# Four of the eight w2_out operand pairs are converted between the attention stages, and output stores are issued two steps later

## The chip, the cores and the metric

The kernel runs on one core of a Trainium2 chip. The metric is the time of one execution on the device in microseconds (us). Five engines matter here: TensorE (PE, with its weight loads shown apart as PEld), VectorE (DVE), ScalarE (ACT), the queue that issues most transfers (SP), and the 16 DMA engines that carry them. Each engine takes its instructions in the order in which they stand in its own queue, and waits for others by semaphores.

## The reference, cut to what matters

```python
# attention through 32 memory slots (4 batches, 8 heads, 576 positions, 64 wide)
a = exp(phi - max(phi, axis=2)); a = a / (sum(a, axis=2) + 1e-9)
k_m = einsum('bhsm,bhsd->bhmd', a, k); v_m = einsum('bhsm,bhsd->bhmd', a, v)
attn = softmax(q @ k_m.T / 8)            # over the 32 slots
x = (attn @ v_m) laid out as 2304 x 512
# gated layer: 512 -> 1536 -> 512
x = ((x @ w_a) * (x @ w_b)) @ w_out
# leaky layer: 512 -> 2048 -> 512
h = x @ w2_in
return maximum(0.01 * h, h) @ w2_out     # 2304 x 512, fp32
```

## The kernel before, in words

All products run as fp32r passes on TensorE: each operand is split into a high and a low part, and three of the four products of parts are summed. A weight tile of 128 rows is loaded into one of five staging tiles (`stage0` to `stage4`, `NS = 5`), two ACT instructions (lines 263 and 267) and one DVE instruction (line 275) bring it into fp32, and ACT and DVE then make the high and the low part.

**First phase, planned.** Its steps are collected in a `Plan` (line 41): each has an engine, a cost in us, what it must follow, and perhaps a staging tile or a PSUM bank that it takes and gives back. `order` (line 79) simulates the engines and puts the steps into one order by due time; `early` makes a step due earlier. The order fixes every engine's queue, SP's included. The phase has eight units: the four batches with the first six column blocks of the gated layer, then the four with the other six. A unit is 144 matmuls `ab` (line 793), a few `wp` (line 742), and 144 matmuls `x1p` (line 850). The attention of batch b+1 (ten small matmul groups with DVE and ACT work between them) lies inside the `x1p` of unit b, so units 0 to 2 hold the attention stages of batches 1 to 3. Units 4 to 7 also hold conversions of the second layer's weights.

**Second phase, in program order and then scheduled.** Both products of the leaky layer are made by a 7-product scheme on 2x2 blocks. Its operands (sums and differences of blocks, with high and low part) are made by `plan_pair` (line 930): "in" pairs from `w2_in`, "out" pairs from `w2_out`, eight of each. A pair loads two weight tiles, converts them, forms four sums, splits seven operands, and stores them in four parts to a scratch area in DRAM (line 1014). The second phase reads them back: `h` matmuls (line 1241, six per step) take `ring` tiles (line 1048), `o` matmuls (line 1330, nine per step) take `w2o` tiles (line 1303) through staging tiles, two halves in each, up to six steps ahead.

The 2304 rows and 16 blocks give 24 quads of `h` products, in six chunks of 28 steps. Chunk 0 has `h` alone; in chunks 1 to 5 a step is six `h` matmuls of the chunk and nine `o` matmuls of the chunk before; a last chunk has `o` alone. Its final product, 36 matmuls, stands on line 1311. ACT and DVE take each `h` result out of PSUM (lines 1258 to 1272), form the sums `g` (line 1284) and split them into `S` (lines 1293 and 1294).

In the kernel before, the eight "in" pairs and the first four "out" pairs are in the plan (units 4 to 7); the last four "out" pairs (`LATE = 4`) are not. A second small plan, `late_plan` (line 1372), orders their steps, and the loop over the second phase emits them step by step beside chunks 0 and 1:

```python
tempo += 0.9
while late and late[0].start < tempo:
    late.popleft().emit()
```

They use staging tiles for the loads and the tiles `R0`, `R1`, `B4` and `G5` for the results. Until they are done, `w2o` has two of its four staging tiles, `S` four of its seven places. An output block is stored (line 1364) as soon as its sum stands; each store is six transfers on SP.

Of the kernel before, what the change touches and what calls it, by code (L numbers as in the profile page):

```python
# [176 lines left out]
def kernel(  # L177
# [39 lines left out]
    NP = NM // 2  # L217
# [6 lines left out]
    LATE = 4  # L224
# [69 lines left out]
    def plan_conv(c, before, users, due=1e9):  # L294

        h = Hold("stage", 1)
        load = plan.add(DMA, 1.46, lambda: c.load(f"stage{h.place}"), take=h)
# [14 lines left out]
    def plan_wab(f):  # L312

        pair = f // 2
        if f % 2 == 0:
            wab_slot[pair] = plan.slot(f"A{pair % NA}")
        for n, src in enumerate((w_a, w_b)):

            def make(n=n):
                if pair not in wab_t:  # L320
                    wab_t[pair] = keep.tile([128, KD, 2, 2, 128], F32, tag=f"A{pair % NA}", name="wab")
                return wab_t[pair][:, :, f % 2, n, :]

            view = src[:, f * 128:(f + 1) * 128].rearrange("(t p) c -> p t c", p=128)
            plan_conv(Conv(("wab", f, n), view, make, 1), *wab_slot[pair])

    def plan_wo(f):
# [6 lines left out]
        plan_conv(Conv(("wo", f), w_out[f * 128:(f + 1) * 128, :], make, 2), before, users)  # L334
# [10 lines left out]
    def plan_att(b):  # L345
# [155 lines left out]
        for g in range(NG):  # L501
# [22 lines left out]
            for n in range(2):  # L524
# [30 lines left out]
                else:  # L555
# [6 lines left out]
                    vb_end[b, g] = add(DVE, t_dve(128), values, [s_kvt], give=[hold_t], early=5.0 if b else 0.0)  # L562
# [123 lines left out]
        for i in range(3):  # L686
# [24 lines left out]
            ends += [s_hi, add(DVE, t_dve(384), low, [s_hi], give=[hold], early=5.0)]  # L711
# [165 lines left out]

    units = [(b, range(f, f + FH)) for f in (0, FH) for b in range(B)]
    n_first = B

# [6 lines left out]
    for u, (b, fs) in enumerate(units):  # L887
# [29 lines left out]
    OPS = (("A11", "B11"), ("S2", "T2"), ("A12", "B21"), ("S3", "T3"), ("S1", "T1"), ("A22", "T4"), ("S4", "B22"))  # L917
    PARTS = (("A11", "S2"), ("A12", "S3"), ("S1", "A22"), ("S4",))
    scr = ctx.enter_context(tc.tile_pool(name="scratch", bufs=1, space=bass.MemoryType.DRAM))
    a_scr, o_scr, a_kept = {}, {}, {}  # L920

    O_OPS = (("A11", "B11", "y"), ("S3", "T3", "z"), ("S2", "T2", "y"), ("A22", "T4", "z"), ("S1", "T1", "y"),
             ("A12", "B21", "x"), ("S4", "B22", "z"))
    O_PARTS = (("B11", "T3"), ("T2", "T4"), ("T1", "B21"), ("B22",))
    IN_SUMS = ((("S1", (1, 0), (1, 1), ALU.add), ("S2", "S1", (0, 0), ALU.subtract)),
               (("S3", (0, 0), (1, 0), ALU.subtract), ("S4", (0, 1), "S2", ALU.subtract)))
    OUT_SUMS = ((("T1", (0, 1), (0, 0), ALU.subtract), ("T2", (1, 1), "T1", ALU.subtract)),
                (("T3", (1, 1), (0, 1), ALU.subtract), ("T4", (1, 0), "T2", ALU.subtract)))

    def plan_pair(plan, kind, mp, due, places=("R0", "R1")):  # L930

        c, js = {}, []
        inner = kind == "in"
        sums, parts, letter = (IN_SUMS, PARTS, "A") if inner else (OUT_SUMS, O_PARTS, "B")
        names = [x for ops in sums for op in ops for x in op[1:3] if not isinstance(x, str)]
        names += [(int(x[1]) - 1, int(x[2]) - 1) for part in parts for x in part if x[0] == letter]
        holds = [Hold("stage", sum(x[0] == i for x in names)) for i in range(2)]
        convs = []
        for i in range(2):
            m = 2 * mp + i  # L940
            if inner:
                view = w2_in[:, m * 128:(m + 1) * 128].rearrange("(t p) c -> p t c", p=128)
            else:
                view = w2_out[m * 128:(m + 1) * 128, :]
            conv = Conv(("w2" + kind, m), view, None, 2)
            convs.append(conv)
            load = plan.add(
                DMA, 1.46, lambda conv=conv, h=holds[i]: conv.load(f"stage{h.place}"), [s_p2], take=holds[i], due=due
            )
            v = plan.add(ACT, t_act(512), conv.high_word, [load])  # L950
            z = plan.add(ACT, t_act(512), conv.low_word, [load])
            js.append(plan.add(DVE, t_dve(512), conv.join, [v, z]))

        def a(i, k):
            w = convs[i].hw.bitcast(F32)
            if inner:
                return w.rearrange("p (a k c) -> p a k c", a=2, k=2)[:, :, k]
            return w[:, 256 * k:256 * k + 256].rearrange("p (a c) -> p a c", a=2)

        def src(op):  # L960
            if op in c:
                return c[op]
            return a(int(op[1]) - 1, int(op[2]) - 1)

        made = {}
        for n, ops in enumerate(sums):
            before, users = plan.slot(f"ob{n}")
            for i, (name, x, y, op) in enumerate(ops):

                def add(name=name, x=x, y=y, op=op, n=n, i=i):  # L970
                    if i == 0:
                        c["t", n] = keep.tile([128, 2, 2, 128], F32, tag=f"ob{n}", name="S")
                    x, y = (c[z] if isinstance(z, str) else a(*z) for z in (x, y))
                    c[name] = c["t", n][:, i]
                    dve.tensor_tensor(out=c[name], in0=x, in1=y, op=op)

                need = [made[z] for z in (x, y) if isinstance(z, str)]
                give = [holds[z[0]] for z in (x, y) if not isinstance(z, str)]
                uses = [users] + [made[z].users for z in (x, y) if isinstance(z, str) and made[z].users is not users]
                made[name] = plan.add(DVE, t_dve(256), add, js + before + need, give=give, uses=uses)  # L980
                made[name].users = users
        for i, part in enumerate(parts):
            tag = f"X{i}" if inner else places[i % len(places)]
            before, users = plan.slot(tag)
            lows = []
            for o, name in enumerate(part):

                def parted(o, x, i=i):
                    t = c["out", i][:, o]
                    return t[:, :, x] if inner else t[:, x].rearrange("p (a c) -> p a c", a=2)  # L990

                def high(i=i, o=o, name=name, tag=tag, part=part, parted=parted):
                    if o == 0:
                        shape = [128, len(part), 2, 2, 128] if inner else [128, len(part), 2, 256]
                        pool = p2[0] if tag[0] in "XR" else keep
                        c["out", i] = pool.tile(shape, F32R, tag=tag, name="a_out" if inner else "w2o")
                    act.activation(out=parted(o, 0), in_=src(name), func=ACTF.Copy)

                def low(o=o, name=name, parted=parted):
                    dve.tensor_tensor(out=parted(o, 1), in0=src(name), in1=parted(o, 0).bitcast(F32), op=ALU.subtract)  # L1000

                direct = name[0] == letter
                need = js if direct else [made[name]]
                uses = [users] if direct else [users, made[name].users]
                hi = plan.add(ACT, t_act(256), high, need + before + lows, uses=uses)
                lows.append(plan.add(
                    DVE, t_dve(256), low, [hi], uses=uses, give=[holds[int(name[1]) - 1]] if direct else ()
                ))

            def store(i=i, part=part):  # L1010
                shape = [128, len(part), 2, 2, 128] if inner else [128, len(part), 2, 256]
                t = scr.tile(shape, F32, tag=f"{kind}{mp}_{i}", name="a_scr")
                (a_scr if inner else o_scr)[mp, i] = t
                dma.dma_start(out=t, in_=c["out", i].bitcast(F32))

            kept = plan.add(DMA, 0.73 * len(part), store, lows, uses=[users], due=due)
            if inner:
                a_kept[mp, i] = kept
        return holds

    for mp in range(NP):
        due = clock[0] - 20.0 + 2.0 * mp
        plan_pair(plan, "in", mp, due)
        if mp < NP - LATE:
            plan_pair(plan, "out", mp, due + 6.0)
# [473 lines left out]
```

## Time and profile before

| what | value |
|---|---|
| time, median of 3 executions | 771.82 us (771.09 to 773.05) |
| profiled execution, its own time | 773.19 us |
| its span, first to last instruction | 771.4 us |
| granted TensorE clock, mean | 0.997 |
| PE busy | 753.5 us (98%) |
| PEld busy | 709.5 us (92%) |
| DVE busy | 549.4 us (71%) |
| ACT busy | 424.0 us (55%) |
| DMA, mean | 227 GB/s |

The profiled execution took 1.37 us more than the median; 1.8 us of its time lie outside the span. The first `h` matmul starts at 397.16 us, the second phase takes the rest. Busy shares are means over stages with different limits, so the stages have to be read apart.

### The profile page before, as it was taken

What the parts mean: (1) busy time and instruction counts of PE and PEld (TensorE: products, weight loads), DVE (VectorE), ACT (ScalarE), POOL (GpSimd) and SP (SyncE); (2) the same over time, 40 slices, a digit from 0 to 9 for tenths busy, and PEclk for the clock granted to TensorE, in tenths of its full rate; (3) what the DMA queues carried; (4) which work ended last, traced back from release to release, by engine and by line L of the source; (5) the groups of instructions that cost most, each with busy time, mean ns of one, the idle gap of its engine ahead of it and who ended that gap; (6) DMA issues with size and microseconds to landing.
All of it is one profiled execution on the core that took longest, in us unless ns stands there. A gap on an engine that the chain in (4) does not pass through costs nothing.

```text
span 771.4 us, 16541 instructions
## 1 busy us (share of the span) xinstructions
PE 753.5 (98%) x6462; PEld 709.5 (92%) x6462; DVE 549.4 (71%) x1082; ACT 424.0 (55%) x894; POOL 1.2 (0%) x9
## 2 busy tenths in 40 slices
PE   8999999999999999999999999999999999999996
PEld 5599899898998989898998899999999999999995
DVE  5794764646828988997987767976755966756683
ACT  4897444544948676666665455633444733444440
POOL 0000000000000000000000000000000000000000
PEclk9999999999999999999999999999999999999998
DMA  9986305102705877679759999987897777886375
GB/s 305 350 289 230 102 2 187 31 2 82 237 13 164 285 275 278 215 250 342 266 202 308 285 361 331 332 268 234 277 311 251 254 249 241 266 318 211 124 235 133
DMA packets 86925, 175.41 MB, mean 227 GB/s; under 512 B 8000, under 2 KB 35136, under 8 KB 86848
## 3 DMA queue, kind: packets, MB, share of 16 engines
q1 hardware_dynamic: 86608, 174.16, 66.9%
q8 instruction: 51, 0.84, 0.4%
q10 hardware_dynamic: 240, 0.20, 0.1%
q14 instruction: 26, 0.21, 0.1%
HBM read 140.25 MB, written 34.08 MB: 226 GB/s over the span
## 4 chain that ended last, share of the span: by engine, by line
PE 88%; DMA 6%; ACT 2%; DVE 2%; SPq 1%; issue 1%; ACTq 0%; DVEq 0%
PE o L1330 22%; PE ab L793 20%; PE h L1241 19%; PE x1p L850 18%; PE wp L742 3%; DMA stage<-in_moe_w_out_dram 2%; DMA w2o<-a_scr 2%; DMA stage<-in_moe_w_a_dram 1%; PE sc L625 1%; PE km L481 1%; DMA a_scr<-w2o 1%; PE qT L597 1%; PE warm L1179 1%; PE o L1311 1%; SPq L1364 1%
## 5 line engine op out<-in xcount | busy, mean ns | idle before, releaser
L1330 PE MATMUL o<-w2o,S 128*128 128x256 f32 x1476 | 196.8, 282 | 1.7 <-DMA w2o<-a_scr 1.7
L1330 PEld LDWEIGHTS o<-w2o,S 128*128 128x128 f32 x1476 | 191.7, 190 | 2.3 <-DMA w2o<-a_scr 2.3
L793 PEld LDWEIGHTS ab<-AT,W 128*128 128x128 f32 x1152 | 153.9, 188 | 14.4 <-issue 5.9
L850 PE MATMUL x1p<-G,wo 128*128 128x288 f32 x1152 | 164.3, 298 | 0.0
L850 PEld LDWEIGHTS x1p<-G,wo 128*128 128x128 f32 x1152 | 154.7, 188 | 6.7 <-issue 3.0
L793 PE MATMUL ab<-AT,W 128*128 128x288 f32 x1152 | 159.2, 297 | 1.0 <-DVE W L761 0.7
L1241 PE MATMUL h<-T,ring 128*128 128x384 f32 x720 | 144.3, 337 | 2.8 <-ACT g L1251 1.6
L1294 DVE TENSOR_TENSOR S<-g,S 128x384 fp32r<-128x384 f32 x168 | 92.6, 556 | 73.5 <-ACT S L1293 73.1
L1293 ACT ACTIVATE S<-g 128x384 fp32r<-128x384 f32 x168 | 87.2, 521 | 102.1 <-PE o L1330 99.6
L1241 PEld LDWEIGHTS h<-T,ring 128*128 128x128 f32 x720 | 121.5, 189 | 5.0 <-ACT g L1251 2.5
L1241 PE MATMUL h<-B,ring 128*128 128x384 f32 x288 | 58.7, 338 | 1.7 <-ACT sums L1258 1.6
L815 DVE TENSOR_TENSOR g<-a_sb,ab 128x288 f32<-128x288 f32 x96 | 42.9, 452 | 20.7 <-PE ab L793 15.8
L1284 DVE TENSOR_TENSOR g<-g 128x384 f32<-128x384 f32 x96 | 52.4, 554 | 3.4 <-ACT g L1251 2.4
L263 ACT ACTIVATE stage<-stage 128x512 f32<-128x512 f32 x68 | 46.4, 683 | 13.6 <-DMA stage<-in_moe_w_out_dram 8.3
L1241 PEld LDWEIGHTS h<-B,ring 128*128 128x128 f32 x288 | 48.3, 188 | 3.0 <-ACT sums L1258 2.3
L810 ACT COPY a_sb<-ab 128x288 f32<-128x288 f32 x96 | 38.0, 396 | 15.1 <-PE ab L793 14.3
L267 ACT ACTIVATE stage<-stage 128x512 int32<-128x512 uint32 x68 | 46.1, 678 | 0.0
L761 DVE TENSOR_TENSOR W<-wp,W 128x512 fp32r<-128x512 f32 x48 | 32.4, 687 | 18.7 <-ACT W L755 17.9
L829 ACT ACTIVATE G<-g 128x576 fp32r<-128x576 f32 x48 | 32.9, 686 | 18.3 <-DVE g L815 18.3
L833 DVE TENSOR_TENSOR G<-g,G 128x576 fp32r<-128x576 f32 x48 | 36.2, 755 | 7.8 <-ACT G L829 7.3
L755 ACT ACTIVATE W<-wp 128x512 fp32r<-128x512 f32 x48 | 27.8, 597 | 24.3 <-PE wp L742 14.8
L1351 DVE TENSOR_TENSOR C<-C,o 128x768 f32<-128x768 f32 x32 | 30.2, 953 | 12.6 <-PE o L1330 11.7
(108 smaller groups left out, 658.6 us busy)
## 6 DMA issues: line engine op xcount, KB each, us to landing
w2o<-a_scr SPq DMA_DIRECT2D x168, 256.0 KB, 4.0
ring<-a_scr SPq DMA_DIRECT2D x72, 512.0 KB, 5.1
stage<-in_moe_w_out_dram SPq DMA_DIRECT2D x28, 512.0 KB, 5.7
a_scr<-a_out SPq DMA_DIRECT2D x24, 512.0 KB, 5.5
a_scr<-w2o SPq DMA_DIRECT2D x24, 512.0 KB, 5.3
stage<-in_moe_w_in_dram SPq DMA_DIRECT2D x16, 512.0 KB, 4.9
stage<-in_moe_w_a_dram SPq DMA_DIRECT2D x12, 512.0 KB, 5.6
stage<-in_moe_w_b_dram SPq DMA_DIRECT2D x12, 512.0 KB, 5.7
```

The source lines that it names most:

```text
L263: act.activation(out=x, in_=x, func=ACTF.Prelu, scale=2.0 ** -112, alpha=2.0 ** 32)
L267: act.activation(out=self.lw, in_=self.lw.bitcast(U32), func=ACTF.Copy, scale=7.249 / 2.0 ** 32, bias=0.25)
L793: pe.matmul(out=c[x, n][:, :HS], lhsT=W[b, f][:, hw, g, 128 * x:128 * x + 128], rhs=AT[b][:, g, ha, n * HS:(n + 1) * HS], start=(g == 0 an ...
L810: act.copy(c["sb"][:, n], c[0, n][:, :HS])
L815: dve.tensor_tensor(out=c["g"][:, n], in0=c["sb"][:, n], in1=c[1, n][:, :HS], op=ALU.mult)
L833: dve.tensor_tensor(out=t[:, 1], in0=c["g"], in1=t[:, 0].bitcast(F32), op=ALU.subtract)
L850: pe.matmul(out=c[n][:, :HS], lhsT=wo_t[f][:, hw, 128 * m:128 * m + 128], rhs=G[b, f][:, hg, n], start=(f == fs[0] and (hw, hg) == PASSES[0]),
L1241: pe.matmul(out=out, lhsT=ring[i % 2, part][:, o, kp, hw], rhs=x[:, hx], start=fresh and kp == 0 and (hw, hx) == PASSES[0], stop=kp == 1 a ...
L1284: dve.tensor_tensor(out=t, in0=x, in1=y, op=op)
L1293: act.activation(out=t[:, 0], in_=src, func=ACTF.Copy)
L1294: dve.tensor_tensor(out=t[:, 1], in0=src, in1=t[:, 0].bitcast(F32), op=ALU.subtract)
L1330: pe.matmul(out=acc[chain][:, 256 * u:256 * u + 256], lhsT=s[:, hs, 128 * u:128 * u + 128], rhs=t[:, ht], start=fresh and q == 0 and u != ...
```

## The change

`LATE`, `late_plan` and the emission beside the second phase are gone. The "out" pairs 4 and 5 are planned in unit 1 and the pairs 6 and 7 in unit 2, right behind the unit's `ab` steps, with the unit's `x1p` as due time. Their results take staging tiles too (a `Hold` on the pool "stage" that is given back when the store has landed). Each of these pairs follows the last store of the one before; the first follows the end of the attention of its batch. The second half of `w_a`, `w_b` and `w_out` follows the last of these stores. Two `early` values rise from 5 to 8 us. In the second phase `w2o` has four staging tiles (eight halves) and `S` seven places from the beginning. An output block's stores go into a queue and are issued two steps of the loop later.

```diff
-    LATE = 4
-            load = plan.add(DMA, 1.46, lambda: c.load(f"stage{h.place}"), take=h)
+            load = plan.add(DMA, 1.46, lambda: c.load(f"stage{h.place}"), after, take=h)
...
-  vb_end[b, g] = add(DVE, t_dve(128), values, [s_kvt], give=[hold_t], early=5.0 if b else 0.0)
+  vb_end[b, g] = add(DVE, t_dve(128), values, [s_kvt], give=[hold_t], early=8.0 if b else 0.0)
...
-  ends += [s_hi, add(DVE, t_dve(384), low, [s_hi], give=[hold], early=5.0)]
+  ends += [s_hi, add(DVE, t_dve(384), low, [s_hi], give=[hold], early=8.0 if b else 5.0)]
...
         for i, part in enumerate(parts):
-            tag = f"X{i}" if inner else places[i % len(places)]
-            before, users = plan.slot(tag)
+            hold = Hold("stage", 1) if soon else None
+            tag = None if soon else f"X{i}" if inner else f"R{i % 2}"
+            before, users = ([], []) if soon else plan.slot(tag)
...
+    SOON_AT = {1: (4, 5), 2: (6, 7)}
+    SOON = [mp for mps in SOON_AT.values() for mp in mps]
...
+        for mp in SOON_AT.get(u, ()):
+            soon = plan_pair("out", mp, clock[0], att_end[b, 1, 1] + soon[-1:], True)
...
-                        plan_wab(f)
+                        plan_wab(f, soon[-1:])
...
-                plan_wo(f)
+                plan_wo(f, soon[-1:])
...
-        if done and not first:
-            store_out(c // 2, done)
+        if done and not first:
+            stores.append((2, c // 2, done))
...
+            for _ in range(len(stores)):
+                wait, *what = stores.popleft()
+                if wait:
+                    stores.append((wait - 1, *what))
+                else:
+                    store_out(*what)
...
-            if late:
-                tempo += 0.9
-                while late and late[0].start < tempo:
-                    late.popleft().emit()
```

**ACT where the second phase begins.** `sums` and `g` on the left are results of `h` matmuls, taken out of PSUM; `S` is their split; `w2o` is a result of an "out" pair. Before, from the first copy of an `h` result on:

```order
L1258 COPY sums<-h 128x384
L997 ACTIVATE w2o<-stage 128x256
L997 ACTIVATE w2o<-S 128x256
L1258 COPY g<-h 128x384
L997 ACTIVATE w2o<-S 128x256 x2
L997 ACTIVATE w2o<-stage 128x256
L1251 ACTIVATE g<-h 128x384
L1293 ACTIVATE S<-g 128x384
L997 ACTIVATE w2o<-S 128x256
L997 ACTIVATE w2o<-stage 128x256
L1251 ACTIVATE g<-h 128x384
```

And now, at the same place:

```order
L1267 COPY sums<-h 128x384
L1267 COPY g<-h 128x384
L1260 ACTIVATE g<-h 128x384
L1302 ACTIVATE S<-g 128x384
L1260 ACTIVATE g<-h 128x384
L1302 ACTIVATE S<-g 128x384
L1260 ACTIVATE g<-U_5594 128x384
L1260 ACTIVATE g<-U_5596 128x384
L1260 ACTIVATE g<-sums 128x384
L1260 ACTIVATE g<-g 128x384
```

No conversion stands any more between the instructions that free PSUM for the next `h` matmuls; the same holds for DVE.

**ACT in the `ab` part of unit 2.** `a_sb` is an `ab` result, `G` the gated product's high part, `W` the next weight. Before:

```order
L810 COPY a_sb<-ab 128x288 x2
L829 ACTIVATE G<-g_1968 128x576
L755 ACTIVATE W<-wp 128x512
L810 COPY a_sb<-ab 128x288 x2
L755 ACTIVATE W<-wp 128x512
```

Now:

```order
L809 COPY a_sb<-ab 128x288 x2
L754 ACTIVATE W<-wp 128x512
L828 ACTIVATE G<-g_2043 128x576
L262 ACTIVATE stage<-stage 128x512
L266 ACTIVATE stage<-stage 128x512
L809 COPY a_sb<-ab 128x288
L262 ACTIVATE stage<-stage 128x512
L266 ACTIVATE stage<-stage 128x512
L754 ACTIVATE W<-wp 128x512
L809 COPY a_sb<-ab 128x288 x2
L958 ACTIVATE w2o<-stage 128x256
```

The two conversions of pair 6 (L262, L266, each waiting for its load) stand ahead of the second block's copies.

**SP at the end of the program.** `w2o` rows are the last operand loads, `out_dram` rows the stores of finished blocks, six transfers each, the last nine for two blocks. Before:

```order
L1303 DMA w2o<-a_scr 128x512 x31
L1364 DMA out_dram<-C 64x256 x6
L1303 DMA w2o<-a_scr 128x512 x2
L1364 DMA out_dram<-C 64x256 x6
L1303 DMA w2o<-a_scr 128x512 x2
L1364 DMA out_dram<-C 64x256 x9
```

Now:

```order
L1312 DMA w2o<-a_scr 128x512 x31
L1375 DMA out_dram<-C 64x256 x6
L1312 DMA w2o<-a_scr 128x512 x3
L1375 DMA out_dram<-C 64x256 x6
L1312 DMA w2o<-a_scr 128x512
L1375 DMA out_dram<-C 64x256 x9
```

One of the four last loads has moved ahead of the second group of stores; the very last one still stands behind twelve stores.

## Rows read from the trace of the kernel before

**Rows 1.** Windows: busy time of each engine in stretches (us), clock, DMA share, GB/s.

```profile
core 0: us, PE busy (x) PEld busy (x) DVE busy (x) ACT busy (x) POOL busy (x), PEclk, DMA share, GB/s
86.00:137.00 51.00, 51.00 (x590) 47.72 (x591) 29.80 (x57) 23.35 (x52) 0.00 (x0) 1.00 0.24 83
137.00:189.00 52.00, 52.00 (x604) 47.63 (x603) 31.78 (x60) 23.54 (x53) 0.00 (x0) 1.00 0.07 21
...
397.00:436.00 39.00, 36.33 (x202) 34.15 (x200) 30.89 (x67) 20.19 (x46) 0.00 (x0) 1.00 0.91 306
436.00:475.00 39.00, 35.45 (x243) 33.82 (x243) 24.40 (x52) 20.43 (x44) 0.00 (x0) 1.00 0.96 335
...
513.00:731.00 218.00, 218.00 (x1549) 218.00 (x1548) 147.94 (x269) 97.85 (x196) 0.00 (x0) 1.00 0.76 251
```

**Rows 2.** Waits of PE, whole run: us in total, times, longest us.

```profile
PE o L1311 <- DMA w2o<-a_scr: 3.4, 2, 2.5
PE o L1330 <- DMA w2o<-a_scr: 1.7, 2, 1.2
...
PE h L1241 <- ACT g L1251: 1.6, 2, 1.4
...
PE aT L692 <- DVE AT L707: 0.8, 1, 0.8
```

**Rows 3.** Timeline of PE, 395 to 440: start, us, what, [idle before <-releaser].

```profile
397.16 2.56 PE L1241 MATMUL h<-B,ring 128*128 128x384 f32 x12
...
422.83 7.81 PE L1241 MATMUL h<-T,ring 128*128 128x384 f32 x42 [1.41 <-ACT g L1251]
```

**Rows 4.** Timeline of PE, 684 to 703.

```profile
686.48 1.22 PE L1330 MATMUL o<-w2o,S 128*128 128x256 f32 x9
687.54 1.21 PE L1241 MATMUL h<-B,ring 128*128 128x384 f32 x6
...
701.27 1.22 PE L1330 MATMUL o<-w2o,S 128*128 128x256 f32 x9
```

**Rows 5.** Timeline of ACT, 392 to 440.

```profile
421.03 0.43 ACT L997 ACTIVATE w2o<-stage 128x256 fp32r<-128x256 f32 x1 [4.24 <-DMA a_scr<-w2o]
```

**Rows 6.** ACT's groups by line and shape: xcount | busy us, mean ns | idle before.

```profile
L263 ACT ACTIVATE stage<-stage 128x512 f32<-128x512 f32 x68 | 46.4, 683 | 13.6 <-DMA stage<-in_moe_w_out_dram 8.3 <-DMA stage<-in_moe_w_in_dram 3.1 <-DMA stage<-in_moe_w_a_dram 2.2
L267 ACT ACTIVATE stage<-stage 128x512 int32<-128x512 uint32 x68 | 46.1, 678 | 0.0
...
L997 ACT ACTIVATE w2o<-S 128x256 fp32r<-128x256 f32 x32 | 12.4, 412 | 10.6 <-DVE S L975 8.6 <-DMA a_scr<-w2o 1.6 <-PE x1p L850 0.4
```

**Rows 7.** DVE's groups by line and shape.

```profile
L275 DVE SCALAR_TENSOR_TENSOR stage<-stage 128x512 int32<-128x512 int32 x44 | 30.3, 689 | 4.9 <-ACT stage L267 4.7
...
L1000 DVE TENSOR_TENSOR w2o<-S,w2o 128x256 fp32r<-128x256 f32 x32 | 12.8, 422 | 0.9 <-ACT w2o L997 0.8
```

**Rows 8.** DMA issues, 60 to 260: xcount, KB each, median us to landing.

```profile
stage<-in_moe_w_b_dram SPq DMA_DIRECT2D x4, 512.0 KB, 4.5
...
a_scr<-w2o SPq DMA_DIRECT2D x1, 512.0 KB, 3.6
```

**Rows 9.** Timeline of SP's queue, 60 to 260.

```profile
136.81 0.88 SPq L369 DMA_DIRECT2D phi_t<-in_phi_dram  x2
186.43 0.37 SPq L256 DMA_DIRECT2D stage<-in_moe_w_b_dram  x1
```

**Rows 10.** Timeline of all engines, 745 to 772.

```profile
744.82 13.04 PE L1330 MATMUL o<-w2o,S 128*128 128x256 f32 x108
...
754.06 1.03 SPq L1303 DMA_DIRECT2D w2o<-a_scr  x2
...
755.17 4.39 SPq L1364 DMA_DIRECT2D out_dram<-C  x6
...
759.66 1.02 SPq L1303 DMA_DIRECT2D w2o<-a_scr  x2
...
762.88 4.75 PE L1311 MATMUL o<-w2o,S 128*128 128x256 f32 x24 [2.50 <-DMA w2o<-a_scr]
```

More of the change, by code (lines that the diff above doesn't have):

```diff
@@ L292, with plan_conv @@
     conv_end = {}
-    def plan_conv(c, before, users, due=1e9):
+    def plan_conv(c, before, users, due=1e9, after=()):
         h = Hold("stage", 1)
-        load = plan.add(DMA, 1.46, lambda: c.load(f"stage{h.place}"), take=h)
+        load = plan.add(DMA, 1.46, lambda: c.load(f"stage{h.place}"), after, take=h)
         loads[c.key] = load
@@ L332, in make @@
             return t[:, 0], t[:, 1]
-        plan_conv(Conv(("wo", f), w_out[f * 128:(f + 1) * 128, :], make, 2), before, users)
+        plan_conv(Conv(("wo", f), w_out[f * 128:(f + 1) * 128, :], make, 2), before, users, after=after)
     AT, vblk = {}, {}
@@ L924 @@
[L924 to L982, printed above, removed]
-            tag = f"X{i}" if inner else places[i % len(places)]
-            before, users = plan.slot(tag)
[L985 to L1019, printed above, removed]
@@ L1197 @@
     two["Q"], two["Z"] = t[:, 0], t[:, 1]
-    places = [i for i in range(NS) if i != s4.place]
     units = deque()
@@ L1206 @@
     u_place(f"AT{B - 1}", 6)
-    for i in range(FH - 1):
+    for i in range(FH):
         u_place(f"G{i}", 3)
@@ L1217, in s_place @@
         s_slots.append(pool.tile([128, 2, TB], F32R, tag=tag, name="S"))
-    s_place(keep, f"B{FH - 1}")
+    for pool, tag in ((keep, f"B{FH - 2}"), (keep, f"B{FH - 1}"), (p2[0], "R0"), (p2[0], "R1")):
+        s_place(pool, tag)
     def t_place(i):
@@ L1223, in t_place @@
         t_slots.extend((t[:, 0], t[:, 1]))
+    for i in range(NS):
+        if i != s4.place:
+            t_place(i)
     w_sets = [
@@ L1366, in store_out @@
                 )
-    class Late(Plan):
-        def add(self, engine, cost, emit, after=(), uses=(), **kw):
-            return super().add(engine, cost, emit, [x for x in after if x is not s_p2], uses, **kw)
-    late_plan = Late(stage=0)
-    late_plan.places["stage"] = [(0.0, i) for i in places]
-    for mp in range(NP - LATE, NP):
-        late_holds = plan_pair(late_plan, "out", mp, 100.0 * mp, ("R0", "R1", f"B{FH - 2}", f"G{FH - 1}"))
-    late = deque(late_plan.order())
-    def late_steps(until):
-        while late and late[0].start < until:
-            late.popleft().emit()
     quads = [(r, mp) for r in range(NTB // 2) for mp in range(NP)]
@@ L1441 @@
                 o_ready(c - 1, k)
-            elif k == steps - AHEAD:
-                for i in places:
-                    if i not in [h.place for h in late_holds]:
-                        t_place(i)
             if c < chunks:
@@ L1455 @@
                 advance(now, T_AHEAD, load_t, t_slots)
-            if late:
-                tempo += 0.9
-                while late and late[0].start < tempo:
-                    late.popleft().emit()
-                if not late:
-                    for h in late_holds:
-                        t_place(h.place)
-                    for pool, tag in ((p2[0], "R0"), (p2[0], "R1"), (keep, f"B{FH - 2}")):
-                        s_place(pool, tag)
-                    u_place(f"G{FH - 1}", 3)
         if c == 0:
```

108 lines of the change are left out of this document (95 added, 13 removed).

## The prediction

> **What bounds the kernel now.** TensorE does nearly all of the time, so I look for the stretches in which it does not work at its own pace. I read four views, in this order.
>
> First the windows [rows 1]. From 513 to 731 us PE and PEld are both busy all 218.00 us: nothing waits there, and no change in DVE, ACT or DMA can shorten it. From 397 to 475 us, the first 78 us of the second phase, PE misses 2.67 and 3.55 us, PEld 4.85 and 5.18 us, and the DMA engines are 0.91 and 0.96 busy, against 0.76 later. The units with attention (86 to 189) keep PE full; DVE there is idle 51.00 - 29.80 = 21.2 and 52.00 - 31.78 = 20.2 us, ACT 27.7 and 28.5 us, DMA 0.24 and 0.07 busy.
>
> Which of the two PE rows tells the loss? The Trainium skill, Perfetto Trace Analysis, section "Identifying the Most-Contended Engine", says that matmul busy time is a poor measure because matmuls are pipelined, and that the weight loads' busy share should be used. By PE's row the loss would be 6.2 us, by PEld's 10.0 us; the count that follows agrees with the second.
>
> Second, the pace [rows 4]. In the undisturbed stretch seven steps take 701.27 - 686.48 = 14.79 us, 2.113 us each; nine `o` matmuls take 1.06 us of it, six `h` matmuls 1.05 us. At this pace the second phase is 28 x 1.05 = 29.4 us (chunk 0), 140 x 2.113 = 295.8 us and 28 x 1.06 = 29.7 us, together 354.9 us. The first `h` matmul starts at 397.16 [rows 3], so PE would end at 752.1. It ends at 762.88 + 4.75 = 767.63 [rows 10]: 15.5 us are lost. The `o` matmuls of line 1330 end at 744.82 + 13.04 = 757.86 [rows 10]; without the last 36 matmuls (4 x 1.06 = 4.2 us) they would have ended at 747.9. So 10.0 us are lost before the tail, which by [rows 1] lie between 397 and 475, and 5.5 us in the tail.
>
> Third, PE's waits [rows 2] and ACT [rows 5]. The longest waits of `h` are for ACT's line 1251, and the longest of these, 1.41 us at 422.83 [rows 3], follows directly from ACT: at 421.03 it starts a late conversion for which it had stood 4.24 us, because the result tile's earlier store had not landed. Behind that instruction in ACT's queue stood the copies that free PSUM for PE. The `o` matmuls wait 1.7 us for `w2o` loads, in the stretch where these have two staging tiles instead of four.
>
> Fourth, the tail [rows 10]. Two loads are issued at 754.06, then six stores take SP from 755.17 to 759.56, and only at 759.66 come the last two loads. PE goes on at 762.88.
>
> **The work that moves.** One "out" pair is, on ACT, four conversions of 0.68 us and seven high parts of 0.41 us [rows 6]: 2.7 + 2.9 = 5.6 us; on DVE, two joins of 0.69 us and eleven operations (four sums, seven low parts) of 0.42 us [rows 7]: 1.4 + 4.6 = 6.0 us. In transfers it is two loads of 512 KB, three stores of 512 KB and one of 256 KB. Four pairs: 22.4 us of ACT, 24.0 us of DVE, 11 MB. None of it disappears; all of it leaves the stretch from 397 to 475 and goes in halves to the units 1 and 2.
>
> **Step 1, the hand-over to the second phase.** With the conversions gone, ACT's and DVE's queues hold only what frees PSUM and makes operands, `w2o` has eight halves and `S` seven places from the start, and SP has no store of a conversion between ring loads. The next 218 us show that this mix runs without loss. Bounds: all of the 10.0 us come back, or none. I take a remainder of 1.2 us, one wait of the size of those in [rows 2]: chunk 0 has two quads at a time, an order that no undisturbed stretch shows, and what is late next would be the sums `g` at the end of chunk 0. Term: -8.8 us.
>
> **Step 2, what the units 1 and 2 pay.** Each gets 12.0 us of DVE work into 21.2 and 20.2 idle us, and 11.2 us of ACT work into 27.7 and 28.5 [rows 1]. The cover is there on average, but the engines take their queues in order. In unit 2 the first load of pair 6 can be issued behind the `phi` loads, at 136.81 + 0.88 = 137.7 us [rows 9]; with 4.5 us to landing [rows 8] it is there at 142.2, and its conversion stands in ACT's queue ahead of the second block's copies, which come at about that time. Behind the waiting conversion are `a_sb` copies and `G`, and PE waits for them only when all four PSUM banks are full. The Trainium skill, DMA: Bandwidth & Descriptors, section "Anatomy of one DMA — SWDGE (gpsimd) path", gives for that path a fixed 2 us plus bytes over 436 GB/s, an estimate of 3.2 us for 512 KB; by that figure the load would land at 140.9, nothing would wait and the term would be 0. The trace does not agree, 4.5 us against 3.2 us, and the trace decides. Bounds: nothing (below it a gain is excluded as PE is full in these windows, except for the 0.8 us that it waits for DVE's AT [rows 2], in a part whose order stays), and at worst an exposed wait as long as the longest of [rows 5], 4.24 us, for each of the four pairs, 17 us. I take 0.8 us, what the attention stages show now [rows 2], because it is the nearest row. Term: +0.8 us.
>
> The other moves cost nothing. All twelve later `w_a` and `w_b` loads now stand on SP behind the last of these stores; seven of them were issued from 186.43 on before [rows 9], and five earlier ones only held staging tiles until then. They need a place in SP's queue some 5 us earlier than the first conversion, and pair 7 is done by the middle of unit 2's `x1p`. If this cover were gone, the next user is unit 4, over 30 us later. The loads for attention on SP's queue pass stores that wait for DVE; their users are a unit away. The planned pairs of units 4 to 7 are the same as before. The higher `early` values only move attention ahead in unfilled queues.
>
> **Step 3, the tail.** The order decides. The first store group stands where it stood; then three loads instead of two follow (754.06 to about 755.6 at 0.51 us each), then the second group, 4.39 us, and the last load at about 760.2, where it was before. What changes is that three of four operands have landed then, so 18 instead of 24 matmuls remain behind the last wait: six matmuls at 4.75 / 24 = 0.198 us [rows 10], 1.2 us gained, less 0.5 us by which the wait now ends with the fourth load and not the third. Bounds: the whole 5.5 us, or 0.5 us lost. Term: -0.7 us.
>
> **Sum.** -8.8 + 0.8 - 0.7 = -8.7 us. The profiled execution's 773.19 us become 764.5. It lay 1.37 us over the median of 771.82, so I predict 763.1 us.
>
> **Rivals.**
>
> *The wait is only exchanged* (17%). DMA is 0.91 to 0.96 busy in the stretch; if ring and `w2o` loads, not the queues, set its pace, or if the first chunk's sums on DVE do, half of the 10.0 us stays. For it: `o` waits for loads [rows 2]. Against it: 11 MB go away from a stretch that carries 25 MB (321 GB/s over 78 us, as the mean of 306 and 335 [rows 1]), which leaves less than the 251 GB/s that the loss-free stretch carries. Price: -5.0 + 0.8 - 0.7 = -4.9, 766.9 us.
>
> *Slower* (5%): ACT stands in front of the moved loads in the units 1 and 2 and takes the `ab` results with it. Place: the conversions of the pairs 4 to 7 between the `a_sb` copies. Price: 4.24 us for each of four pairs, 17 us, against 10.0 - 1.2 + 0.7 = 9.5 us gained, +7.5 us: 779 us. It decides from 2.4 us exposed per pair on. Against it: the copies of an `ab` block have three more banks in hand, and only pair 6 is near its load.
>
> *The stores do all that they could* (6%): the last load gets ahead of the second store group on the chip and the tail's 5.5 us go: 763.1 - 4.8 = 758.3 us. The order speaks against it.
>
> *No effect* (5%): the moved work exposes about what the hand-over gives back, within 2.3 us of 771.8. Against it: DVE and ACT are over a third idle there.
>
> *Forecast* (67%): 760.5 to 766 us.
>
> **Range and chances.** 0.3% is 2.3 us, about what a measurement of this kernel can tell from no change. Up to 768.5 us the range takes in the exchanged wait; down to 760.0 it takes in a hand-over without remainder. What is left out is slower, no effect and most of the stores' case, some 15%. Faster 0.90, same 0.05, slower 0.05.
>
> **What the new profile would show.** Step 1: between 397 and 475 PEld misses under 3 us instead of 10.0; no `h` wait on ACT over 1.3 us; DMA under 0.85 there. The step is wrong if PE waits for `g`, `sums` or `w2o` there for more than 4 us. Step 2: PE still full from 86 to 231, the first `h` matmul at 397 to 399; it is wrong if `ab` waits for `a_sb` or W, and `h` begins after 400. Step 3: the last `w2o` load is issued 2 to 3 us after PE has run out of work, and 18 matmuls follow it; it is wrong if PE's last wait is under 1 us. The forecast as a whole is wrong above 768.5 us.

## The result and the profile after

| | kernel before | changed kernel |
|---|---|---|
| time, median of 4 executions each on one chip | 772.03 us (771.09 to 773.05) | 763.27 us (762.07 to 764.37) |
| ratio, 95% interval | | 0.9886 (0.9863 to 0.9909) |
| profiled execution | 773.19 us, span 771.4 | 764.37 us, span 762.5 |

The changed kernel is 8.8 us faster; 763.1 had been predicted. The windows of the changed kernel answer to [rows 1]; the columns are the same.

```profile
86.00:137.00 51.00, 50.55 (x583) 47.03 (x584) 39.26 (x84) 32.36 (x75) 0.00 (x0) 1.00 0.57 196
137.00:189.00 52.00, 52.00 (x600) 47.19 (x599) 39.45 (x85) 37.43 (x85) 0.00 (x0) 1.00 0.50 175
397.00:436.00 39.00, 39.00 (x240) 38.87 (x239) 25.69 (x49) 16.05 (x32) 0.00 (x0) 1.00 0.67 221
436.00:475.00 39.00, 39.00 (x278) 39.00 (x278) 23.27 (x43) 19.47 (x38) 0.00 (x0) 1.00 0.78 252
513.00:731.00 218.00, 218.00 (x1559) 218.00 (x1558) 150.25 (x274) 98.93 (x198) 0.00 (x0) 1.00 0.78 248
```

The work has moved as planned: DVE and ACT are some 8 to 14 us busier in each of the two attention windows, and from 397 to 475 PEld misses 0.13 us instead of 10.0. In the first attention window PE misses 0.45 us. That is no new loss: it is part of the 0.85 us wait for DVE's AT, which ended at 85.91 us before, just ahead of this window, and ends at 86.45 now. PE's waits, over the whole run, answer to [rows 2]:

```profile
PE o L1320 <- DMA w2o<-a_scr: 2.3, 2, 1.7
PE sc L624 <- ACT kk L551: 1.2, 2, 0.9
PE aT L691 <- DVE AT L706: 0.8, 1, 0.8
```

No wait of `h`, and none of `o` outside the tail, is left. PE's timeline at the hand-over answers to [rows 3]:

```profile
398.48 2.24 PE L1250 MATMUL h<-B,ring 128*128 128x384 f32 x12
...
427.73 1.20 PE L1250 MATMUL h<-B,ring 128*128 128x384 f32 x6
428.77 1.24 PE L1339 MATMUL o<-w2o,S 128*128 128x256 f32 x9
```

The first `o` follows 30.3 us behind the first `h`, and the two go by turns from there. The tail answers to [rows 10]:

```profile
744.76 4.82 PE L1339 MATMUL o<-w2o,S 128*128 128x256 f32 x39
...
745.78 1.49 SPq L1312 DMA_DIRECT2D w2o<-a_scr  x3
...
747.37 3.67 SPq L1375 DMA_DIRECT2D out_dram<-C  x6
...
750.86 1.66 PE L1320 MATMUL o<-w2o,S 128*128 128x256 f32 x12 [0.56 <-DMA w2o<-a_scr]
751.13 0.53 SPq L1312 DMA_DIRECT2D w2o<-a_scr  x1
...
754.25 0.93 PE L1320 MATMUL o<-w2o,S 128*128 128x256 f32 x6 [1.73 <-DMA w2o<-a_scr]
...
755.35 2.93 PE L1320 MATMUL o<-w2o,S 128*128 128x256 f32 x12 [0.17 <-DVE C L1324]
```

Three loads, six stores, one load: as read from the order, 18 matmuls stand behind the last wait. Five points of the program cut the run into pieces that can be compared: the first `x1p`, the first `h`, the end of the last ordinary `o` (here 744.76 + 4.82 = 749.58), the end of PE, the end of the span.

| kernel | first x1p | to first h | to last ordinary o | to PE's end | to span's end | span |
|---|---|---|---|---|---|---|
| before | 55.29 | 341.87 | 360.70 | 9.77 | 3.77 | 771.4 |
| changed | 55.84 | 342.64 | 351.10 | 8.70 | 4.22 | 762.5 |
| difference | +0.55 | +0.77 | -9.60 | -1.07 | +0.45 | -8.9 |

### The profile page after: what moved, and what is told of

Read it like the earlier page. It is cut to its first block, busy times and chain, and to the rows that moved or that the text cites. A ratio compares the mean times of both kernels' runs of the same rounds, so it can differ in the third digit from the quotient of the medians.

```text
span 762.5 us, 16527 instructions
## 1 busy us (share of the span) xinstructions
PE 750.5 (98%) x6462; PEld 709.8 (93%) x6462; DVE 549.1 (72%) x1082; ACT 423.7 (56%) x894; POOL 1.2 (0%) x9
## 4 chain that ended last, share of the span: by engine, by line
PE 95%; DMA 2%; SPq 1%; DVE 1%; ACT 1%; issue 0%; ACTq 0%
PE h L1250 23%; PE o L1339 22%; PE x1p L849 21%; PE ab L792 20%; PE wp L741 3%; DMA stage<-in_moe_w_a_dram 1%; PE sc L624 1%; PE km L480 1%; PE qT L596 1%; PE warm L1184 1%; PE o L1320 0%; SPq L1375 0%; PE aT L691 0%; DMA w2o<-a_scr 0%; DVE AT L706 0%
## 5 line engine op out<-in xcount | busy, mean ns | idle before, releaser
L1250 PE MATMUL h<-T,ring 128*128 128x384 f32 x720 | 142.2, 336 | 0.0
L262 ACT ACTIVATE stage<-stage 128x512 f32<-128x512 f32 x68 | 46.4, 683 | 8.0 <-DMA stage<-in_moe_w_out_dram 3.2
L266 ACT ACTIVATE stage<-stage 128x512 int32<-128x512 uint32 x68 | 46.2, 679 | 0.0
L1260 ACT ACTIVATE g<-U 128x384 f32<-128x384 f32 x36 | 18.8, 522 | 33.4 <-DVE U L1275 23.7
```

Of the source, the lines that this page charges most:

```text
L262: act.activation(out=x, in_=x, func=ACTF.Prelu, scale=2.0 ** -112, alpha=2.0 ** 32)
L266: act.activation(out=self.lw, in_=self.lw.bitcast(U32), func=ACTF.Copy, scale=7.249 / 2.0 ** 32, bias=0.25)
L1250: pe.matmul(out=out, lhsT=ring[i % 2, part][:, o, kp, hw], rhs=x[:, hx], start=fresh and kp == 0 and (hw, hx) == PASSES[0], stop=kp == 1 a ...
```

## The experiments

The second-phase piece (first `h` to last ordinary `o`) is read from each profile. The times come from several chips; each ratio compares with the kernel before on the same chip.

| kernel | piece, us | time, us | ratio to before (95%) |
|---|---|---|---|
| before / changed | 360.70 / 351.10 | 772.03 / 763.27 | 1 / 0.9886 |
| before, stores later | 360.32 | 770.65 | 0.9977 (0.9959 to 0.9996) |
| changed, stores at once | 351.10 | 765.22 | 0.9903 (0.9873 to 0.9933) |
| changed, `early` 5.0 | 351.09 | 764.55 | 0.9892 (0.9861 to 0.9924) |
| changed, GpSimd stores | 351.09 | 759.90 | 0.9836 (0.9808 to 0.9865) |
| changed, 11 MB more on SP | 356.57 | 768.13 | 0.9963 (0.9946 to 0.9981) |
| changed, 6.8 MB more on GpSimd | 351.15 | 763.54 | 0.9888 (0.9865 to 0.9910) |
| changed, more busy time | 351.56 | 763.55 | 0.9900 (0.9861 to 0.9938) |
| changed, landing waits | 353.90 | 767.15 | 0.9929 (0.9909 to 0.9950) |
| two pairs early, two late | 352.61 | 764.04 | 0.9906 (0.9872 to 0.9940) |
| changed, few places | 350.99 | 762.66 | 0.9874 (0.9854 to 0.9893) |
| written order, GpSimd stores | 370.03 | 780.27 | 1.0110 (1.0087 to 1.0134) |
| written order, `o` held back | 371.43 | 787.81 | 1.0195 (1.0173 to 1.0217) |

**The two parts of the change, one at a time.** The kernel before with later stores:

```diff
-            store_out(c // 2, done)
+            stores.append((2, c // 2, done))
```

> The kernel before with one part of the change alone: a store of a finished output block is issued two steps later. The late conversions stay beside the two long matmul stages. Theory (the gain is the conversions taken out of the in-order queues; the delay helps the tail alone): 0.3 to 1.2 us shorter than before, 770.8 to 771.7 us; the loss at the start of the long matmul stretch stays near 10 us and the first products still start near 397. Rival (the stores do all they could, and more than the tail): 4 to 6 us shorter, near 767 us. If the delay does nothing: within 0.3 us of before.

> The changed kernel with its stores issued at once again, as before the change; the early conversions stay. Theory: 0.3 to 1.2 us longer than the changed kernel, 763.6 to 764.5 us, all of it behind the last loads of the second operand: about 5.5 us are lost there instead of 4.5. Rival (the delay carries more than the tail): 4 us or more of the gain is gone, 767 us or longer.

The first run measured 0.23% (0.04 to 0.41) less, 1.8 us (0.3 to 3.2), which does not exclude the theory's 0.3 to 1.2. The second, at 765.22 us, lies above the 764.5 of the theory, but on another chip than the changed kernel, and by the ratios the two cannot be told apart (the intervals overlap). The piece stays at 360.32 with late conversions and at 351.10 without, whatever the stores do: the stores touch the tail alone. PE's end of the first run against that of the changed kernel above:

```profile
763.45 0.94 PE L1311 MATMUL o<-w2o,S 128*128 128x256 f32 x6 [1.73 <-DMA w2o<-a_scr]
764.55 1.68 PE L1311 MATMUL o<-w2o,S 128*128 128x256 f32 x12 [0.16 <-DVE C L1315]
```

The wait is the same 1.73 us, but the last twelve matmuls take 1.68 us here and 2.93 us there. There the granted clock fell:

```profile
755.00:759.00 4.00, 3.11 (x14) 2.64 (x12) 1.05 (x3) 0.00 (x0) 0.00 (x0) 0.57 0.47 109
```

In this window of the changed kernel the mean is 0.57, most of it at the lower of the two levels (1.2 and 2.4 GHz). In the kernel before with later stores the last window has 1.00:

```profile
763.00:768.00 5.00, 2.63 (x18) 2.25 (x18) 1.20 (x3) 0.00 (x0) 0.00 (x0) 1.00 0.52 128
```

What PE did ahead of it is the same in both, twelve matmuls, a wait of 1.73 us, six matmuls. So up to 1.25 us of the tail come and go: of nine profiles with this order of loads and stores, six show 1.66 to 1.69 us for the last twelve and three 2.40 to 2.93. Among tails whose last matmuls were slowed, the piece from the last ordinary `o` to PE's end is 9.77 us (before) and 9.50 (stores at once) against 8.70 (changed), 8.47 (more busy time) and 7.97 (landing waits) with later stores: these are worth 0.8 to 1.8 us.

**The planner offsets.** `early=8.0` back to 5.0 in both places.

> The changed kernel with the two planner offsets for the second unit's small VectorE pieces (8.0) set back to 5.0, as before the change; all else stays. Theory: the cost of the moved work in units 1 and 2 was put at 0.8 us with these offsets; without them those pieces may stand later behind the moved conversions, 0 to 1 us longer than the changed kernel, the first products of the long stretch 0 to 1 us later than 398.5. Rival (the offsets themselves make the 1.3 us that the first phase became longer): 0.5 to 1 us shorter, the first products at 397.2 to 398.

```profile
56.58 1.62 PE L849 MATMUL x1p<-G,wo 128*128 128x288 f32 x11
...
400.01 2.24 PE L1250 MATMUL h<-B,ring 128*128 128x384 f32 x12
```

From the first `x1p` to the first `h` are 343.43 us. In the ten kernels with the moved work as in the change that is 342.36 to 342.77 us, in the two with the old plan 341.87 and 341.93. The moved work costs 0.4 to 0.9 us, and, in this one profile, 0.7 to 1.1 us more without the offsets. The first `h` is later than the theory's 399.5, but 0.74 us of that were there at the first `x1p` already. The rival falls. The time alone (764.55 us) would not have shown it: the first `x1p` starts anywhere from 54.77 to 56.89 us.

**Stores of the last row block on GpSimd's queue.**

```diff
-                queue = act if h and len(us) == 1 else dma
+                queue = (act if h else dma) if len(us) == 1 else nc.gpsimd if r == 2 else dma
```

> The changed kernel with the stores of the last row block (18 transfers; the three on ScalarE's queue stay) issued on GpSimd's queue instead of SyncE's, so that SyncE's last 35 loads of the second operand follow one another. Theory (the tail loss of 4.5 us stands behind the last load, which SyncE issues only after 12 stores of some 0.6 us each): the last load goes out before 745 us, the wait of 1.7 us and those before it vanish, the loss in the tail falls to 0 to 1.5 us, and the kernel is 2.5 to 4.5 us shorter than the changed one, 759 to 761 us. Rival (the tail is bound by the stores' own landing, or GpSimd issues them slowly): 0 to 1 us shorter or even longer, the time then standing behind the end of TensorE, 7 us or more instead of 4.2.

SP's queue, GpSimd's and PE at the end of this kernel:

```profile
729.97 16.42 SPq L1312 DMA_DIRECT2D w2o<-a_scr  x16
```

```profile
743.06 3.23 POOL L1375 DMA_DIRECT2D out_dram<-C  x6 [741.26 <-DVE C L1360]
...
747.33 3.08 POOL L1375 DMA_DIRECT2D out_dram<-C  x6 [1.04 <-DVE C L1360]
...
750.18 4.61 PE L1320 MATMUL o<-w2o,S 128*128 128x256 f32 x36
```

The last load is out at 746.39 (before 745 had been said), the 36 matmuls run without a wait, and the tail piece falls to 4.45 us, from 8.70 in the changed kernel's profile and 7.41 in one of the same order whose last matmuls were not slowed (`early` 5.0). The kernel is 3.4 us faster than the changed one by the medians (0.5% by the ratios), the best of all.

**Is it the traffic?** Late conversions also brought DMA traffic. First, 22 stores of 512 KB on SP, each behind a one-column DVE copy:

```diff
+            dve.tensor_copy(t[:, :1], w[LAST[n]][:, :1])
+            dma.dma_start(out=extra[i], in_=t.unsqueeze(1).to_broadcast([128, 2, 512]))
```

> The changed kernel with 22 extra stores of 512 KB to scratch memory (11 MB, from tiles that are free there, each behind a one-column VectorE copy that fixes its place), issued on SyncE over the first 44 steps of the long stretch. They bring its DMA share there back to that of before (0.87 to 0.95) or above, with no conversions. The measure is the time from the first product h to the end of the last o product beside it: 360.3 to 360.7 us with the late conversions, 351.1 without. Theory (waits and places in the in-order queues made the loss): 351 to 352.6 us, the kernel at most 1.5 us longer than the changed one. Rival (DMA traffic set the pace, the change only lightened it): 356 us or more, the kernel 5 to 9 us longer.

The piece grew by 5.5 us, as the rival had it. But SP's waits from 397 to 480 and PE's timeline show that more than traffic had changed:

```profile
SPq L1391 <- DVE ob L1390: 23.3, 10, 10.8
```

```profile
424.83 0.99 PE L1339 MATMUL o<-w2o,S 128*128 128x256 f32 x7
...
430.31 3.63 PE L1339 MATMUL o<-w2o,S 128*128 128x256 f32 x29
```

The stores stood in SP's queue for their copies, 23.3 us in ten waits, and the framework's scheduler, which sorts the second phase when the program is built, had set another order on TensorE, with 29 `o` matmuls in a row. So the traffic was tried again by itself, with copy and store both on GpSimd:

```diff
+            nc.gpsimd.tensor_copy(t[:, :1], w[LAST[n]][:, :1])
+            nc.gpsimd.dma_start(out=extra[now // 3], in_=t.unsqueeze(1).to_broadcast([128, 2, 512]))
```

> The changed kernel with 13 extra stores of 512 KB to scratch memory (6.8 MB, about what the kernel before moved more between 397 and 475 us: 6.3 MB by the two windows of each), issued from GpSimd's queue, which is empty there; the one-column copy that fixes the place of each is on GpSimd too, so nothing stands in the queues of SyncE, ScalarE or VectorE, and TensorE's order is word for word that of the changed kernel. In the run with 11 MB, SyncE, VectorE and TensorE's order were disturbed as well, so its 5.5 us do not say that traffic did it. From the first h to the end of the last ordinary o: theory (queues, not traffic): 351.1 to 352 us. Rival (traffic): 354 us or more.

```profile
397.00:436.00 39.00, 39.00 (x240) 38.84 (x239) 25.93 (x49) 16.01 (x32) 9.71 (x20) 1.00 0.87 336
436.00:475.00 39.00, 39.00 (x277) 39.00 (x277) 23.27 (x43) 19.63 (x38) 2.61 (x6) 1.00 0.90 312
```

336 and 312 GB/s, as much as the kernel before moved [rows 1], and PE is full: 351.15 us. Traffic of this size is not the cause. What the run on SP lost stays unassigned: it moved more than this one,

```profile
436.00:475.00 39.00, 35.43 (x233) 33.68 (x232) 19.35 (x43) 14.59 (x30) 0.00 (x0) 1.00 1.01 374
```

374 GB/s, and the queues of SP and DVE and TensorE's order were disturbed as well.

**Is it busy time?** 46 operations more on each of ACT and DVE, one per step (the expectation says 45):

```diff
+            act.activation(out=ob[0][:, :TB], in_=src, func=ACTF.Copy)
+            dve.tensor_tensor(out=ob[1][:, :TB], in0=src, in1=src, op=ALU.add)
```

> The changed kernel with 45 extra ScalarE copies and 45 extra VectorE additions of 128x384, each behind a product's result and written to a tile that nothing reads, over the first 46 steps of the long stretch: about the busy time that the late conversions had there (24 us on ScalarE, 25 us on VectorE), without one wait for a landing. From the first h to the end of the last ordinary o: theory (the landing waits that stand in ScalarE's queue made the loss): 351 to 353 us. Rival (the plain busy time of the two engines made it): 356 to 361 us, with TensorE waiting for ScalarE's and VectorE's g as in the kernel before.

```profile
397.00:436.00 39.00, 39.00 (x237) 38.41 (x236) 37.32 (x76) 29.23 (x64) 0.00 (x0) 1.00 0.70 224
```

DVE is busy 37.32 of 39 us here, more than in the kernel before, and PE is full; the piece grew by 0.46 us. The scheduler had moved TensorE's order a little here too (the first `o` 27.4 us behind the first `h` instead of 30.3), so the 0.46 us hold for that order. Busy time that waits for nothing but `h` is not the cause.

**Is it waits for landings?** ACT writes a tile, SP stores it, ACT writes it again, eight times:

```diff
+            act.activation(out=ob[:, :TB], in_=src, func=ACTF.Copy)
+            dma.dma_start(out=extra[4 * c + k // 6], in_=ob[:, :TB])
+            act.activation(out=ob[:, :TB], in_=src, func=ACTF.Copy)
```

> The changed kernel with eight pure landing waits put into ScalarE's queue in the first 52 steps of the long stretch: ScalarE writes a tile from a product's result, SyncE stores it (196 KB), ScalarE writes the tile again and so stands until the store has landed. Little busy time (16 copies, 8 us) and little traffic (1.6 MB) come with it. From the first h to the end of the last ordinary o: theory (a landing wait at the head of ScalarE's queue stops g, and TensorE runs out behind it): 0.5 to 1.4 us lost for each, 355 to 362 us in all. Rivals (busy time or traffic): within 1 us of 351.1.

ACT's waits from 397 to 520, and the two gaps of PE's timeline above 0.5 us up to 480:

```profile
ACT ob L1388 <- DMA extra<-ob: 9.0, 6, 2.3
```

```profile
416.60 1.32 PE L1250 MATMUL h<-T,ring 128*128 128x384 f32 x6 [0.59 <-ACT g L1267]
...
457.60 1.34 PE L1250 MATMUL h<-T,ring 128*128 128x384 f32 x6 [0.99 <-DVE U L1275]
```

2.80 us lost, neither the 4 to 11 us of the theory nor the 1 us of the rivals. Of 9.0 us that ACT stood, TensorE lost about a third. The waits were not quite alone: SP's queue stood 6.4 us from 397 to 475 for the first copies. This is still the costliest of the ingredients put back, and the waits of the kernel before (5.9 us for `a_scr<-w2o` and 1.3 us for a weight tile from 397 to 475) would by that rate be worth 2 us of the 9.6.

**Is it the places that they held?** The changed kernel with two staging tiles and four `S` places until step 46:

```diff
-    for pool, tag in ((keep, f"B{FH - 2}"), (keep, f"B{FH - 1}"), (p2[0], "R0"), (p2[0], "R1")):
-        s_place(pool, tag)
+    s_place(keep, f"B{FH - 1}")
...
+            elif k == steps - AHEAD:
+                for i in stage_places[:2]:
+                    t_place(i)
```

> The changed kernel with the tile places of the kernel before, and without any late conversion: until step 18 of the second round (the 46th in all) five places for S less four, that is three and one, and two staging tiles for the loads of the second operand instead of four, one G tile held back. This is what the late conversions held besides their time in the queues. From the first h to the end of the last ordinary o: theory (the work in the queues): 351.1 to 352 us. Rival (too few places stop the look-ahead of splits and loads): 354 us or more, with waits of o for its loads as in the kernel before (1.7 us in two).

350.99 us: nothing. (The places are four instead of seven; the words on five places in the expectation count them wrongly.)

**A dose.** `SOON_AT = {1: (4, 5)}`, with 6 and 7 emitted beside the second phase as in the kernel before.

> A dose: of the four pairs of column blocks that the change converts early, 4 and 5 stay early, 6 and 7 are converted beside the long stretch as before the change; stores two steps later as in the changed kernel. Theory: the loss goes with the number of late conversions: from the first h to the end of the last ordinary o 354 to 358 us (351.1 with none late, 360.5 with four pairs), the kernel 3 to 6 us longer than the changed one. Rival (a threshold: two pairs still find room between the look-ahead): within 1 us of 351.1. Rival (what was lost was the start of the stretch as such, with any late pair): 359 us or more.

352.61 us, 1.5 us lost where half the dose should have lost half: outside all three ranges, which leave 352.1 to 354 open. PE's longest gap and its first `o`, and the last store of a conversion on SP:

```profile
401.80 1.32 PE L1251 MATMUL h<-T,ring 128*128 128x384 f32 x6 [0.93 <-ACT g L1268]
...
429.50 1.23 PE L1340 MATMUL o<-w2o,S 128*128 128x256 f32 x9
```

```profile
422.76 0.42 SPq L976 DMA_DIRECT2D a_scr<-w2o  x1
```

Two late pairs are through at 422.76, before the first `o`, and nothing is lost later (PEld is busy all 39.00 us from 436 to 475). Four pairs are not; in the kernel before, on PE and on SP:

```profile
401.98 1.32 PE L1241 MATMUL h<-T,ring 128*128 128x384 f32 x6 [1.22 <-ACT g L1258]
...
436.67 2.42 PE L1330 MATMUL o<-w2o,S 128*128 128x256 f32 x18 [0.53 <-DMA w2o<-a_scr]
...
443.58 1.34 PE L1330 MATMUL o<-w2o,S 128*128 128x256 f32 x9 [1.16 <-DMA w2o<-a_scr]
...
447.70 0.44 PE L1241 MATMUL h<-B,ring 128*128 128x384 f32 x1 [1.03 <-ACT sums L1258]
```

```profile
472.14 1.12 SPq L1014 DMA_DIRECT2D a_scr<-w2o  x1
```

Of the seven gaps above 0.2 us (6.16 us), two stand among the `h` ahead of the first `o` (1.22 here, 1.41 in [rows 3]), one right before it (0.53) and four, 3.00 us, beside `o`, where ACT must also split `S` and SP load `w2o`. The gaps are not the whole loss. By PEld's row [rows 1] 4.85 of the 10.0 us are missing from 397 to 436, ahead of the first `o` at 436.67, and 5.18 from there to 475. So about half of what four pairs lose is lost before any `o`, about three times what two pairs lose in all: the loss goes neither with the number of pairs nor only with the overlap with `o`.

**Is it the order on TensorE?** The rows above show one more thing that the change moved: before, `o` starts 39.5 us behind the first `h` and comes in twos (x18); after, 30.3 us behind, one by one. The scheduler set that order, presumably because it saw the conversions; extra instructions moved it in other runs too. To test the order, the second phase was emitted in written order (`with tc.manual_schedule():`), without late conversions, once as it is and once with `o` held back.

> The changed kernel with the last row block's stores on GpSimd's queue, as in the run that gave 759.9 us, and with the order of the long stretch as the code writes it instead of as the framework's scheduler sorts it. Theory (in the changed kernel the scheduler's order is nearly the written one, h and o by turns): within 0.5 us of the run with GpSimd's stores, 351.1 us from the first h to the end of the last ordinary o. Rival (the scheduler's order still hides something): 1 us or more to either side.

> The changed kernel, no late conversions, in written order, with the o products of the second round held back behind the h products as they stand in the kernel before (the first pair of o steps after six h steps instead of one each by turns, later two and four in a row, level again after 28 steps). In the kernel before the framework's scheduler had set this order at compile time, because it saw the late conversions. From the first h to the end of the last ordinary o: theory (what ScalarE's and SyncE's queues hold makes the loss): 351.1 to 352.5 us. Rival (the order on TensorE itself makes the loss, h products in a row run out of their two banks): 354 to 360 us.

The first run is far out on its rival's side, the second beyond both its ranges. In written order the piece is 370.03 us, 18.9 us more than sorted. PE's waits from 397 to 767 in the first:

```profile
PE h L1250 <- DVE sums L1281: 6.3, 8, 1.3
PE h L1250 <- DVE U L1281: 5.9, 7, 2.6
PE h L1250 <- DVE g L1278: 1.6, 1, 1.6
```

TensorE waits for the DVE results that empty its PSUM banks, 13.8 us of the 18.9; sorted, no such wait is there. Yet TensorE's own order is nearly the same in both: compared with the run with GpSimd's stores, 2496 of the 2520 `h` and `o` matmuls have the same place in the sequence. Written order also sets the queues of DVE and ACT, and these differ. One place in the written order, DVE's queue and then PE:

```profile
600.96 0.56 DVE L1303 TENSOR_TENSOR S<-g,S 128x384 fp32r<-128x384 f32 x1 [1.29 <-ACT S L1302]
601.44 0.55 DVE L1281 TENSOR_TENSOR sums<-sums,h 128x384 f32<-128x384 f32 x1
...
602.04 1.31 PE L1250 MATMUL h<-B,ring 128*128 128x384 f32 x6 [1.25 <-DVE sums L1281]
```

DVE stands 1.29 us for ACT's half of a split of `S`; the sum that empties the bank stands behind that split in DVE's queue, and TensorE idles 1.25 us. So with the same work and nearly the same order on TensorE, the order in the other queues is worth twice the whole change. Holding `o` back adds 1.4 us to that, but on such a base it does not measure the part of TensorE's order in the kernel before.

**What is shown and what stays open.** Shown is that the late conversions make the loss: without them the piece is 9.2 to 9.6 us shorter, whatever the stores do. How they make it is shown only in part. Put back alone, neither their traffic (0.0), nor their places (-0.1), nor busy time like theirs (0.5) makes it; eight landing waits in ACT's queue make 2.8, two late pairs 1.5. The run in written order shows that places in the in-order queues of DVE and ACT can by themselves cost more than all of this. That they did so in the kernel before is argued, not shown: how much of its loss is place in the queues, landing waits or TensorE's own order was not separated.

## Why the prediction was right

- *Step 1, -8.8.* Measured -9.60 (-9.22 against the kernel with later stores only). The remainder was 0.4 us (351.10 against 354.9 - 4.2 = 350.7), not 1.2: no wait for a sum is left in chunk 0. The loss of 10.0 us counted from the pace was right, PE's own busy row (6.2) too low. But the mechanism was told too simply: the 4.24 us wait of [rows 5] costs the 1.41 us that [rows 3] shows, and landing waits alone, put back, gave only 2.80 us. The eight halves of `w2o` and the seven places of `S`, which the step named beside the queues, carry nothing: with two staging tiles and four places the piece was 350.99 us.
- *Step 2, +0.8.* Measured +0.77 in the pair of profiles, 0.4 to 0.9 over all. The load of pair 6 landed at 144.0 us, not at 142.2, but its conversion stood only 0.51 us for it on ACT, less than the 4.24 of the bound:

```profile
144.01 0.70 ACT L262 ACTIVATE stage<-stage 128x512 f32<-128x512 f32 x1 [0.51 <-DMA stage<-in_moe_w_out_dram]
```

  No `ab` waits for it. (The 3.2 us that the prediction sets beside the trace's 4.5 are for GpSimd's path; these loads go out on SP's queue, so the two do not contradict each other.) That the size fits is luck: 0.8 us was borrowed from the wait for AT, and no recorded wait of PE between 86 and 397 us is longer than before. The loss stands in units 1 and 2 without one: the first `ab` of units 1, 2 and 3 start 0.54, 0.87 and 1.32 us later than before, and the 0.54 were there at the first `x1p` already. One sentence was wrong: the `early` values do not only move attention ahead in unfilled queues; with the old ones the step costs 0.7 to 1.1 us more.
- *Step 3, -0.7.* The order was read rightly: last load 751.13, 1.55 us after the last ordinary `o` (2 to 3 had been said), 18 matmuls behind it. PE's tail piece is 1.07 us shorter and the end behind PE 0.45 longer, -0.6. What the step did not see is that up to 1.25 us of the tail hang on the clock of the last matmuls: in the changed kernel's profile they were slowed, and the -0.6 would have been larger without that. The kernel before with later stores alone is 1.8 us shorter by time.
- *The sum, -8.7.* The spans differ by 8.9 us, the medians by 8.8. So close a fit is in part luck. Step 1 gave 0.8 us more than forecast; 0.55 us went the other way up to the first `x1p`, which no step has and which varies from run to run (54.77 to 56.89 us), and some more in the slowed end.
- *Rivals.* "Only exchanged" fell with the 0.4 us that remain of 10.0, and the traffic run excludes the loads' pace as the cause. "No effect" fell with the 8.8 us. "Slower" fell with the 0.51 us. "The stores do all" fell with the order, and the run with GpSimd's queue shows what it would have given: the tail piece 4.25 us shorter than in the changed kernel's profile, about 3 us where the end was not slowed.

## What to carry to other kernels

Count a stretch's loss against the pace of an undisturbed stretch of the same work, and place fixed points in the program; pieces between them repeat to a few tenths while whole runs scatter by 2 us. Here background work beside a full TensorE cost little as busy time or traffic. As work that stands in the same in-order queues as the instructions that empty PSUM, two pairs cost 1.5 us and four 9.2 to 9.6, so move it to a stage whose queues have room, and read there that no wait grows. When a run is meant to test one engine's order, check that the other engines' order stays. Look at what stands in front of the last load on its queue, and give stores there a queue of their own.

## What the runs showed of the hardware

- DMA at 336 and 312 GB/s (0.87 and 0.90 busy) beside a TensorE whose busy row misses nothing.
- The same last twelve matmuls in 1.66 to 1.69 us or in 2.40 to 2.93 us, with the two windows shown at a granted clock of 1.00 and of 0.57, and in these two kernels after the same waits of 1.73 us and 0.16 or 0.17.
- Six stores of 64 KB take GpSimd 3.08 to 3.23 us to issue, SP 3.67 us (4.39 in the kernel before); a load of 256 KB takes SP 0.5 us, or 1.03 us each in a row of sixteen that waits for PE to give tiles free.
